# Three conv quarters exchange their tanh halves through SyncE's queue and take one in-place sum; eleven late buffers; new orders

## The chip, the cores and the metric

The kernel runs on one core of a Trainium2 chip. The metric is the device time of one execution in microseconds; the value of a version is the median over its runs. A profile is one execution recorded by the hardware profiler, with its own time beside the others.

## The reference

Pooled-key attention for 8 batches of 8 heads, then a gated feed-forward layer with a convolution of three taps along the sequence.

```python
B, H, S, D = q.shape                      # 8, 8, 576, 64
k_p = k.reshape(B, H, S // 8, 8, D).mean(axis=3)
v_p = v.reshape(B, H, S // 8, 8, D).mean(axis=3)
scores = np.matmul(q, k_p.transpose(0, 1, 3, 2)) / np.sqrt(D)
attn = softmax(scores)                    # over the 72 pooled keys
x = np.matmul(attn, v_p)                  # -> [B, S, 512]
h = np.maximum(x @ w_in, 0.0)             # [B, S, 1024]
conv_out = sum(conv_w[k] * shifted(h, k - 1) for k in range(3))
gate = 1.0 / (1.0 + np.exp(-conv_out))
out = (h * gate) @ w_out                  # float32
```

## The kernel before, in words

Batches are handled in four groups of two. Each batch goes through the same stages: its keys and values are pooled by sums, its queries are turned; its attention runs in tiles of 128 rows (scores, maximum, shift, exponential, a turn of the weights, weighted values, division, a turn of the result); then the feed-forward part runs on 1024 features in eight blocks of 128 features, called fb, and two quarters of four blocks, called f4; then the output is formed in tiles of 128 rows, copied to SBUF and stored.

A block's `ffn_in` gives h in PSUM and `ffn_relu` (ScalarE, L785) writes it to `hT`, of which there are two buffers. The convolution is made in one of two ways. In a quarter of `TAPS` VectorE makes it with two instructions a block (`ffn_tap`, L912), ScalarE squashes the result into `gT` (L922). In the other quarters TensorE makes it with small 64x64 matmuls (`ffn_conv`, L940), two blocks at a time; those come out with the two halves of partitions of one block in each pair exchanged. ScalarE writes the tanh of the straight block into the gate tile `gT` and that of the exchanged block into a helper tile `tg` (`ffn_tanh`, L965).

The sigmoid is made from a tanh with an added one; relu then carries the factor one half. `ffn_gate` adds the one and undoes the exchange: L980 adds it in place to the two straight blocks, and two instructions of 64 partitions (L982) add it while they move one half of `tg` each to the other half of `gT`. Behind that `ffn_times` (L990) multiplies the four blocks of the gate by h, which frees that part of `hT`. In a tap quarter nothing is exchanged, and a single instruction over four blocks (`ffn_tap_gate`, L927) adds the one; in batches 5 to 7 (`SIG`) ScalarE gives the sigmoid itself and no one is added.

The order of all work on all engines is written out by hand as a table: every step is an `Op` that is added to a `Graph` with the engines that can do it; `ORDER` lists the steps with the engine chosen for each (and -1 for a fill matmul that computes nothing), `FORMS` chooses between a half-array and a quarter-array form of the q and score matmuls, and `PLACES` picks each tile's buffer. Each engine, and SyncE's queue, then does its steps in that order, each waiting for what it needs.

SyncE's queue carries the loads of the first keys and queries (L300), the turn of the weights of groups 2 and 3 (`att_send`, L702: `eT` from `e`), the turn of the attention's result for batches 4 to 7 (`att_out`, L755: `xT` from `x`), the turn of the queries of group 3 (`q_send`, L554) and most stores (`ffn_store`, L1021). Output tiles of the last group go through "late" buffers, which lie in the memory of the query tiles `qp`.

Of the kernel before, what the change touches and what calls it, by code (L numbers as in the profile page):

```python
# [33 lines left out]
class Graph:  # L34
# [28 lines left out]
    CROSS = ()  # L63
    BY_TILE = ()
# [119 lines left out]
def kernel(  # L184
# [10 lines left out]
    nc = tc.nc  # L195
# [66 lines left out]
    def buf(*key):  # L262
        return buffers[key[0]][tokens[key].slots[0]]
# [1236 lines left out]
```

## Time and profile before

| what | value |
|---|---|
| median of 3 runs | 210.57 us (210.29 to 210.69) |
| the profiled execution | 210.06 us |
| its span, first to last instruction | 208.3 us |
| TensorE busy | 197.2 us (95%) |
| VectorE busy | 190.4 us (91%) |
| ScalarE busy | 174.5 us (84%) |
| GpSimd busy | 45.5 us (22%) |
| mean granted TensorE clock | 0.993 |

The span is shorter than the time by what lies around the first and the last instruction. A share of busy time is a mean over stages with different limits: what a change in one stage is worth is read from that stage. TensorE's ends are modelled, so that a busy TensorE is not TensorE at its peak. PE is TensorE, PEld its weight loads, DVE VectorE, ACT ScalarE, POOL GpSimd, SP SyncE; SPq is SyncE's queue. L numbers are lines of the kernel; in the changed kernel the same lines stand some lines lower (L980 is L982 there, L785 is L787, L990 is L999).

### The profile page before, as it was taken

The page shows a single profiled execution, that of the slowest core. Times are in us where ns is not written, and L with a number is a line of the kernel's source. Part 1 is how long each engine was busy: PE and PEld are TensorE (multiplying, and loading weights), DVE is VectorE, ACT ScalarE, POOL GpSimd, SP SyncE. Part 2 cuts the span into 40 slices and gives each one's busy share as a digit, 9 for nine tenths or more (in the row PEclk, how much of TensorE's full clock was granted, in tenths as well). Part 3 has the DMA queues.
Part 4 walks back from the last instruction along what each step waited for, and adds up shares of the span by engine and source line. Part 5 has one row for each costly group of instructions (what it writes and reads, how often), then busy time and mean ns, then how long its engine had stood idle before and what let it go on. Part 6 is the DMA issues. An engine that isn't in the chain of part 4 may idle for free.

```text
span 208.3 us, 6540 instructions
## 1 busy us (share of the span) xinstructions
PE 197.2 (95%) x2650; PEld 134.3 (64%) x2666; DVE 190.4 (91%) x338; ACT 174.5 (84%) x363; POOL 45.5 (22%) x74
## 2 busy tenths in 40 slices
PE   4999999999999999999999999999999999999990
PEld 2568688776688887666868875566556666644450
DVE  7979999889999999999999999999999999999440
ACT  3558786998899999998998999999999999797310
POOL 8553035010173211010000152040234315000000
PEclk9999999999999999999999999999999999999997
DMA  6999999999999999998497465565665557044395
GB/s 205 243 204 209 205 207 208 208 209 203 189 167 202 205 207 206 170 162 164 92 144 123 97 136 111 119 138 127 129 139 116 120 124 179 3 101 102 92 282 185
DMA packets 48835, 33.48 MB, mean 161 GB/s; under 512 B 28300, under 2 KB 43812, under 8 KB 48804
## 3 DMA queue, kind: packets, MB, share of 16 engines
q0 software_dynamic: 15216, 15.40, 45.1%
q1 hardware_dynamic: 32592, 16.20, 36.4%
q10 hardware_dynamic: 996, 1.45, 2.6%
q8 instruction: 21, 0.34, 0.6%
q14 instruction: 10, 0.08, 0.1%
HBM read 32.52 MB, written 9.44 MB: 201 GB/s over the span
## 4 chain that ended last, share of the span: by engine, by line
PE 49%; DVE 24%; ACT 16%; issue 5%; DMA 3%; SPq 0%; DVEq 0%; ACTq 0%
PE psum L776 19%; PE psum L998 13%; DVE tg L912 6%; DVE negm L634 4%; ACT x L739 4%; PE psum L718 3%; DVE gT L990 3%; DVE sd L646 3%; DMA hT<-in_k_dram 3%; PE psum L940 2%; ACT hT L785 2%; PE psum L693 2%; PE psum L608 2%; ACT gT L922 2%; ACT qT L560 2%
## 5 line engine op out<-in xcount | busy, mean ns | idle before, releaser
L776 PE MATMUL psum<-xT,w_in_sb 128*128 128x288 bf16 x512 | 70.6, 286 | 0.4
L998 PE MATMUL psum<-w_out_sb,gT 128*128 128x512 bf16 (+1 forms) x280 | 65.9, 373 | 1.1 <-issue 0.2
L776 PEld LDWEIGHTS <-w_in_sb 128*128 128x128 bf16 x512 | 48.4, 98 | 15.6 <-issue 0.6
L785 ACT ACTIVATE hT<-psum 128x576 bf16<-128x576 f32 x64 | 41.6, 671 | 4.8 <-PE psum L776 4.2
L998 PEld LDWEIGHTS <-gT 128*128 128x128 bf16 x296 | 27.7, 98 | 27.5 <-DVE gT L990 0.6
L860 POOL COPY hT<-hT 128x126 bf16<-128x126 bf16 x14 | 11.3, 810 | 84.2 <-issue 43.6
L912 DVE SCALAR_TENSOR_TENSOR tg<-hT,ratio 128x576 f32<-128x576 bf16 x36 | 28.2, 813 | 0.5 <-ACT gT L922 0.2
L634 DVE TENSOR_REDUCE negm<-psum 128x8 f32<-128x576 f32 (+2 forms) x37 | 27.4, 748 | 1.3 <-PE psum L608 0.6
L912 DVE SCALAR_TENSOR_TENSOR tg<-hT,ratio,tg 128x576 f32<-128x576 bf16 x36 | 28.2, 810 | 0.0
L922 ACT ACTIVATE gT<-tg,ratio 128x576 bf16<-128x576 f32 x36 | 27.4, 793 | 0.8 <-DVE tg L912 0.7
L990 DVE TENSOR_TENSOR gT<-gT,hT 128x2304 bf16<-128x2304 bf16 x16 | 21.4, 1348 | 0.1
L739 ACT ACTIVATE x<-psum,r 128x64 bf16<-128x64 f32 x96 | 21.2, 356 | 0.1
L1009 ACT COPY osb<-psum 128x512 f32<-128x512 f32 x27 | 16.4, 620 | 4.3 <-PE psum L998 2.7
L646 DVE TENSOR_TENSOR sd<-psum,negm 128x576 f32<-128x576 f32 x27 | 19.8, 747 | 0.1
L683 ACT ACTIVATE e<-sd 128x576 bf16<-128x576 f32 x27 | 19.4, 719 | 0.1
L718 PE MATMUL psum<-vm,eT 128*128 128x65 bf16 (+5 forms) x240 | 18.8, 222 | 0.2 <-DVE vm L516 0.2
L718 PEld LDWEIGHTS <-eT 128*128 128x128 bf16 (+1 forms) x240 | 14.8, 101 | 3.6 <-issue 0.8
L746 DVE TENSOR_TENSOR x<-psum,r 128x512 bf16<-128x512 f32 (+1 forms) x25 | 16.6, 679 | 0.2
L425 PE MATMUL psum<-gT 128*128 128x448 bf16 x40 | 12.7, 425 | 2.8 <-DVE gT L1107 2.8
L940 PE MATMUL psum<-hT,dw 64*64 64x63 bf16 (+2 forms) x448 | 13.2, 255 | 0.2 <-ACT kT L505 0.2
L512 DVE TENSOR_TENSOR v<-v 128x1280 bf16<-128x1280 bf16 (+2 forms) x24 | 12.9, 539 | 0.2
L940 PEld LDWEIGHTS <-dw 64*64 64x64 bf16 x448 | 10.9, 107 | 2.1 <-issue 1.5
(94 smaller groups left out, 236.5 us busy)
## 6 DMA issues: line engine op xcount, KB each, us to landing
out_dram<-osb SPq DMA_DIRECT2D x54, 128.0 KB, 2.4
v<-in_v_dram POOLq DMA_DIRECT2D x8, 512.0 KB, 13.7
qp<-in_q_dram POOLq DMA_DIRECT2D x7, 576.0 KB, 13.2
kk<-in_k_dram POOLq DMA_DIRECT2D x3, 1152.0 KB, 14.4
out_dram<-qp ACTq DMA_DIRECT2D x10, 128.0 KB, 3.4
hT<-in_k_dram SPq DMA_DIRECT2D x2, 576.0 KB, 5.0
w_in_sb<-in_moe_w_in_dram POOLq DMA_DIRECT2D x2, 512.0 KB, 15.4
w_out_sb<-in_moe_w_out_dram POOLq DMA_DIRECT2D x1, 1024.0 KB, 18.6
```

Source lines behind the costliest of these rows:

```text
L634: nc.vector.tensor_reduce(out=a["m"][0:rows], in_=a["s"][0:rows, :, 0:2 * KW].rearrange("p a (h s) -> p a h s", s=Sp), axis=AX.X, op=OP.ma ...
L646: nc.vector.tensor_tensor(out=a["d"][0:rows], in0=a["s"][0:rows, :, 0:2 * KW].rearrange("p a (h s) -> p a h s", s=Sp), in1=a["m"][0:rows]. ...
L683: nc.scalar.activation(out=dst, in_=src, func=ACT.Exp,)
L718: nc.tensor.matmul(out=a["o"][lo:hi, h // 4, (h % 4) * (D + 1):(h % 4 + x1 - x0) * (D + 1)], lhsT=a["eT"][:, j, lo:hi], rhs=buf("vm", b)[: ...
L739: nc.scalar.activation(out=a["x"][0:rows, n * D:(n + 1) * D], in_=ov[:, n // 4, n % 4, 0:D], func=ACT.Identity, scale=r[0:rows, n // 4, n ...
L776: nc.tensor.matmul(out=banks(ps)[:, j, 0:SC], lhsT=w_in_block(dc, fb), rhs=buf("xT", g)[:, dc, i * S + j * SC:i * S + (j + 1) * SC], start ...
L785: nc.scalar.activation(out=h_of(b)[:, fb].rearrange("p (a s) -> p a s", a=2), in_=banks(ps)[:, :, 0:SC], func=ACT.Relu, scale=1.0 if (b, f ...
L912: nc.vector.scalar_tensor_tensor(out=acc, in0=h, scalar=w, in1=acc if tap else mid, op0=OP.mult, op1=OP.add)
L922: nc.scalar.activation(out=gate, in_=acc_of(b, fb, ps), func=squash(b, fb), scale=ratio[:, 1, fb:fb + 1])
L940: nc.tensor.matmul(out=banks(pss[r ^ c])[c * D:(c + 1) * D, j, lo:hi], lhsT=dw[r * D:(r + 1) * D, tap * n_fb + fb, :], rhs=hT[r * D:(r + 1 ...
L990: nc.vector.tensor_tensor(out=gate, in0=gate, in1=h_of(b)[:, four], op=OP.mult)
L998: nc.tensor.matmul(out=bank(ps)[0:rows, columns], lhsT=buf("gT", g)[:, fb, t * P:t * P + rows], rhs=w_out_sb[:, fb, columns], start=(fb == 0),
```

## The change

Three of the quarters that TensorE convolves, (2, 0), (2, 1) and (3, 0) as (batch, quarter), get another gate. The two exchanged halves of `tg` are moved into `gT` by two DMAs on SyncE's queue (`ffn_cross`), as soon as the tanh of both exchanged blocks are written; then `ffn_tap_gate` adds the one to all four blocks in place with one VectorE instruction, behind all four tanh and the DMAs. The four other convolved quarters keep `ffn_gate`. The late buffers grow from 8 to 11, the three new ones in the memory of the value tiles `v`; a copy into a late buffer also waits until the pooled values of batches 4 to 7 are made. `ORDER`, `FORMS` and `PLACES` are new throughout.

```diff
+    SWAP = ((2, 0), (2, 1), (3, 0))
...
     ORDER = (
-        0, 16, 4, 24, 12, 44, 28, 8, 10, 14, 32, -1, -1, 42, 36, -1, -1, 40, -1, -1,
+        0, 16, 4, 24, 8, 12, 44, 48, 14, 42, 10, 64, -1, -1, 3, -1, 32, -1, -1, 38,
...
-             "hT": 2, "gT": 2, "xT": 2, "qT": 3, "kk": 1, "qp": 4, "v": 3, "vm": 5, "kT": 5, "sd": 3, "r": 3, "s": 2, "late": 8}
+             "hT": 2, "gT": 2, "xT": 2, "qT": 3, "kk": 1, "qp": 4, "v": 3, "vm": 5, "kT": 5, "sd": 3, "r": 3, "s": 2, "late": 11}
...
     half_qp = [t.rearrange("p h s -> p (h s)")[:, i * 1024:(i + 1) * 1024] for t in buffers["qp"] for i in range(2)]
+    half_qp += [t.rearrange("p j x -> p (j x)")[:, 0:1024] for t in buffers["v"]]
...
+    def ffn_cross(b, f4):
+        g, i = where[b]
+        tg, gate = buf("tg", b, f4), buf("gT", g)[:, 4 * f4:4 * f4 + 4, i * S:(i + 1) * S]
+        gate = gate.rearrange("p (f e) s -> p e f s", e=2)
+        for r in range(2):
+            nc.sync.dma_start(out=gate[r * D:(r + 1) * D, 1], in_=tg[(1 - r) * D:(2 - r) * D])
...
+            elif f2 % 2 and (b, f4) in Graph.SWAP:
+                o = add({"SP": 1.3}, w, lambda f4=f4: ffn_cross(b, f4), after=[tanh[f4][1], tanh[f4][3]], uses=tg + [gtok[g]], land=(2.4, 0, 1))
+                need = [o] + tanh[f4]
+                if (b, f4) not in Graph.SIG:
+                    need = [add(dve(0.78), w + 6 * f2 + Graph.GATE, lambda f4=f4: ffn_tap_gate(b, f4), after=need, uses=[gtok[g]])]
+                gated = add(dve(1.39), w + 6 * f2 + Graph.GATE, lambda f4=f4: ffn_times(b, f4), after=need, uses=[htok[b], gtok[g]])
+                gdone.setdefault(b, []).append(gated)
...
-            osb, free = (token("late", g, t), [x for n in range(4, B) for x in qdone[n, 0]]) if g == 3 else (token("osb", g, t), [])
+            osb, free = (token("late", g, t), [x for n in range(4, B) for x in qdone[n, 0] + [vdone[n]]]) if g == 3 else (token("osb", g, t), [])
```

Where the tables move the instructions is seen best on three engines. On VectorE, at the gates of batch 3, the order before reads (a row is the line, the operation, out<-in with buffer numbers, and partitions x elements):

```order
L980 TENSOR_SCALAR gT_122<-gT_122 128x2x576
L982 TENSOR_SCALAR gT_122<-tg_118 64x2x576 x2
L731 RECIPROCAL r_113<-psum 128x8
L912 SCALAR_TENSOR_TENSOR tg_119<-hT_116,ratio,tg_119 128x576
L990 TENSOR_TENSOR gT_122<-gT_122,hT_116 128x4x576
L516 TENSOR_TENSOR vm_90<-v_88,mask_wide 128x15x64
L927 TENSOR_SCALAR gT_122<-gT_122 128x4x576
L990 TENSOR_TENSOR gT_122<-gT_122,hT_116 128x4x576
```

and now, for the same batch, whose h lies in the other buffer:

```order
L929 TENSOR_SCALAR gT_122<-gT_122 128x4x576
L514 TENSOR_TENSOR v_89<-v_89 128x5x256
L999 TENSOR_TENSOR gT_122<-gT_122,hT_117 128x4x576
L733 RECIPROCAL r_113<-psum 128x8
L748 TENSOR_TENSOR x_107<-psum,r_113 128x512
L636 TENSOR_REDUCE negm_95<-psum 128x8
L929 TENSOR_SCALAR gT_122<-gT_122 128x4x576
L648 TENSOR_TENSOR sd_129<-psum,negm_95 128x576
L733 RECIPROCAL r_113<-psum 128x8
L748 TENSOR_TENSOR x_110<-psum,r_113 128x512
L999 TENSOR_TENSOR gT_122<-gT_122,hT_117 128x4x576
```

The tap quarter now comes first and the exchanged quarter, with its single sum, second, and attention work stands between the sum and the product. On SyncE's queue, around the second turn of queries, the order before reads:

```order
L554 DMA_TRANSPOSE qT_79<-qp_76 128x18x128
L1021 DMA out_dram<-osb_126 64x512 x2
L755 DMA_TRANSPOSE xT_114<-x_107 128x4x128
L702 DMA_TRANSPOSE eT_104<-e_103 128x5x128
L702 DMA_TRANSPOSE eT_105<-e_101 128x5x128
L755 DMA_TRANSPOSE xT_114<-x_110 128x4x128
L554 DMA_TRANSPOSE qT_80<-qp_75 128x18x128
L702 DMA_TRANSPOSE eT_104<-e_102 128x5x128
```

and now:

```order
L556 DMA_TRANSPOSE qT_80<-qp_74 128x18x128
L704 DMA_TRANSPOSE eT_106<-e_101 128x5x128
L556 DMA_TRANSPOSE qT_81<-qp_77 128x18x128
L993 DMA gT_122<-tg_118 64x2x576 x2
L704 DMA_TRANSPOSE eT_104<-e_102 128x5x128
L757 DMA_TRANSPOSE xT_114<-x_109 128x4x128
L757 DMA_TRANSPOSE xT_114<-x_108 128x4x128
L757 DMA_TRANSPOSE xT_114<-x_107 128x4x128
L704 DMA_TRANSPOSE eT_105<-e_103 128x5x128
L993 DMA gT_122<-tg_120 64x2x576 x2
```

The two turns of queries stand closer together, and the first exchange (L993) is right behind the second. On ScalarE, where the next batch's first relu goes into the buffer that batch 3 leaves, the order before reads:

```order
L965 ACTIVATE gT_122<-psum 128x576
L785 ACTIVATE hT_116<-psum 128x576
L683 ACTIVATE e_101<-sd_129 128x2x2x144
L965 ACTIVATE tg_120<-psum 128x576
L965 ACTIVATE gT_122<-psum 128x576
```

and now:

```order
L787 ACTIVATE hT_116<-psum 128x576
L787 ACTIVATE hT_117<-psum 128x576
L967 ACTIVATE gT_122<-psum 128x576
L967 ACTIVATE tg_119<-psum 128x576
L787 ACTIVATE hT_117<-psum 128x576
```

In both the relu into the freed buffer stands ahead of the last two tanh of batch 2.

More of the change, by code (lines that the diff above doesn't have):

```diff
@@ L72 @@
     ORDER = (
[55 rows of a table removed]
[55 rows of a table added]
     )
     FORMS = (
-        1, 1, 1, 0, 0, 1, 1, 0, 0, 0, 1, 1, 0, 1, 1, 0, 0, 0, 1, 1, 1, 0, 1, 1, 1, 0, 0, 1, 0, 1, 0, 1, 1, 1, 1, 1, 1, 1, 0, 0,
+        1, 0, 1, 0, 0, 1, 1, 0, 0, 0, 1, 1, 1, 0, 0, 0, 0, 0, 1, 1, 0, 0, 1, 0, 0, 0, 0, 1, 1, 0, 0, 1, 0, 0, 0, 1, 1, 0, 1, 0,
     )
     PLACES = (
[18 rows of a table removed]
[18 rows of a table added]
     )
```

144 rows, old and new, of tables (ORDER, PLACES) are left out of this document.

## The prediction

> **What bounds the kernel now.** I read the page's head first, then busy time by stretch, then the chain of waits.
>
> ```profile
> span 208.3 us, 6540 instructions
> ...
> PE 197.2 (95%) x2650; PEld 134.3 (64%) x2666; DVE 190.4 (91%) x338; ACT 174.5 (84%) x363; POOL 45.5 (22%) x74
> ```
>
> The columns of the stretches are: length, then busy time and (instructions) of PE, PEld, DVE, ACT and POOL, the granted clock, the DMA share, GB/s.
>
> ```profile
> 47.00:95.00 48.00, 47.36 (x797) 34.81 (x799) 47.35 (x84) 45.65 (x90) 9.93 (x20) 1.00 1.17 191
> 95.00:128.00 33.00, 32.56 (x497) 23.94 (x499) 32.62 (x59) 31.05 (x72) 4.65 (x8) 1.00 0.67 121
> 128.00:154.00 26.00, 25.69 (x248) 15.59 (x251) 26.00 (x42) 25.86 (x69) 5.49 (x8) 1.00 0.59 126
> 154.00:194.00 40.00, 39.58 (x247) 23.73 (x250) 39.59 (x53) 36.47 (x77) 8.21 (x8) 1.00 0.48 106
> ```
>
> From 47 to 194 us VectorE is busy 47.35 + 32.62 + 26.00 + 39.59 = 145.56 of 147 us: 1.44 us idle in all. TensorE reads 145.19 of 147, but its ends are modelled. ScalarE is full only in 128 to 154 (25.86 of 26). Outside this stretch VectorE has slack only ahead of 47 us.
>
> ```profile
> 1.83 6.32 DMA hT<-in_k_dram
> 8.17 1.16 ACT kk L307
> 9.37 0.75 PE psum L432 x18
> ...
> 148.57 1.31 ACT x L739 x4
> ...
> 182.80 8.83 DVE tg L912 x12
> 191.63 2.55 DVE gT L990 x2
> 194.23 8.84 PE psum L998 x48
> ```
>
> The chain (start, length, what) begins with the load of the first keys and their cast, passes ScalarE's divides (L739) around 148 us, and ends in the last twelve taps, two products and the 48 matmuls that need those products. After 203.07 us only a copy and stores follow. So the end stands where VectorE's last product stands (194.18), plus a tail of 14.1 us that the change can hardly touch: five tiles need the last product in both versions. What VectorE does before that product, and how long it waits, decides the time.
>
> **The change part by part.** The three quarters first.
>
> ```profile
> L980 DVE TENSOR_SCALAR gT<-gT 128x1152 bf16<-128x1152 bf16 x7 | 3.3, 465 | 0.0
> ...
> L982 DVE TENSOR_SCALAR gT<-tg 64x1152 bf16<-64x1152 bf16 x14 | 6.4, 455 | 0.2
> ...
> L927 DVE TENSOR_SCALAR gT<-gT 128x2304 bf16<-128x2304 bf16 x3 | 2.2, 748 | 0.0
> ```
>
> By busy time over count, a quarter's gate was one L980 and two L982, 3.3/7 + 2 x 6.4/14 = 1.39 us; it becomes one L927, 2.2/3 = 0.73. Three quarters: -1.97 us of VectorE, all of it between 103 and 121 us, where VectorE is full. That is the gain on the path, if nothing takes its place.
>
> Something does. The new order gives VectorE work that was ScalarE's.
>
> ```profile
> L746 DVE TENSOR_TENSOR x<-psum,r 128x512 bf16<-128x512 f32 x23 | 15.3, 679 | 0.2
> L771 DVE COPY xT<-psum 128x512 bf16<-128x512 bf16 x1 | 0.4, 426 | 0.6 <-PE psum L763 0.6
> L707 DVE COPY eT<-psum 128x640 bf16<-128x640 bf16 x3 | 1.4, 477 | 0.0
> L307 DVE CAST kk<-hT 128x1152 bf16<-128x1152 f32 x1 | 0.9, 921 | 0.0
> L739 ACT ACTIVATE x<-psum,r 128x64 bf16<-128x64 f32 x96 | 21.2, 356 | 0.1
> L771 ACT COPY xT<-psum 128x512 bf16<-128x512 bf16 x16 | 9.1, 587 | 1.6 <-PE psum L763 1.5
> ```
>
> VectorE gets one divide more (15.3/23 = 0.67), three full xT copies (3 x 0.4) and a half one (some 0.3), and one raw cast of 512 columns (0.9 x 512/1152 = 0.4): +2.6. It loses one eT copy (1.4/3 = 0.47) and a half-width q copy (about the same): -0.9. Net of the gates, 2.6 - 0.9 - 1.97 = **-0.3 us** of VectorE work ahead of the last product. With errors of a tenth or so in each of eight items I hold it for anything between -0.6 and +0.3.
>
> ScalarE loses eight divide pieces (8 x 21.2/96 = 1.77), three xT copies (3 x 9.1/16 = 1.71) and smaller pieces on both sides that cancel: about -3.3 us. It does not set the end by itself, so this is worth only what VectorE and TensorE waited for it. In the full stretch VectorE has 1.44 us of waits altogether. I take a fifth of them, **-0.3**; the ends are -1.44 (all waits go) and the rivals below (new ones come).
>
> The head: the second half of the first keys is cast on VectorE (0.92) where the chain shows ScalarE's 1.16: **-0.2**. It is worth that only if VectorE is free at 8.17 us, and nothing if it is not.
>
> ```profile
> 2.49 0.24 DVE L1107 MEMSET gT<- 128x224 uint32 x1
> ...
> 7.07 1.15 DVE L382 COPY mask_wide<-mask 128x960 bf16<-128x960 bf16 x1
> ```
>
> ```profile
> 2.79 5.15 PE L425 MATMUL psum<-gT 128*128 128x448 bf16 x14 [2.79 <-DVE gT L1107]
> ```
>
> One thing speaks against the head. The widened mask (L382, 1.15 us) now stands ahead of the clearing (L1107) that the first fill matmuls wait for, so they start some 1.2 us later, and there are 8 and not 14. The 14 took 5.15 us, 0.37 each, though the granted clock reads full there:
>
> ```profile
> PEclk9999999999999999999999999999999999999997
> ```
>
> ```profile
> 73.06 0.38 PE psum L425 x2
> ```
>
> Later fills of the same shape step at 0.38/2 = 0.19 on the chain. If eight fills leave TensorE as quick as fourteen did, this costs 0; if the first transposes and key matmuls run at the slow step, 34 of them lose some 0.05 each up to 9 us, most of it ahead of the second cast, and at most 0.4 us reaches the path. I take 0. The Trainium skill, in "TensorE: Matmul & The Clock Gate", Part 1: The HAM clock gate, says that the first 3.4 us or so of matmuls run at half clock whatever their number, in a window that runs free of the kernel; by that rule the start of full speed moves with the first fill and the sum would be 0.4 worse. The fill's slow steps agree with that; the granted clock row does not show it.
>
> TensorE gets more work: two q transposes change from the small to the full form, six tiles of scores likewise.
>
> ```profile
> L608 PE MATMUL psum<-kT,qT 64*64 64x72 bf16 x408 | 8.1, 200 | 0.2
> ...
> L542 PE MATMUL psum<-ident,qp 128*64 128x128 bf16 x126 | 4.6, 220 | 0.1
> ...
> L621 PE MATMUL psum<-kT,qT 128*128 128x144 bf16 x40 | 4.3, 226 | 0.4 <-ACT e L683 0.3
> ...
> L546 PE MATMUL psum<-ident,qp 64*64 64x64 bf16 x180 | 2.5, 195 | 0.0
> ```
>
> A set of 36 L546 costs 2.5/5 = 0.5, its 18 L542 4.6/7 = 0.66; a tile of 16 L608 0.32, its four L621 0.43: 2 x 0.16 + 6 x 0.11 = +1.0 us. By the order most of it falls before 110 us, where fill matmuls still pad TensorE's gaps, so I cost it at nothing; if TensorE is what the middle waits for, it costs the whole 1.0.
>
> The exchange itself: six issues on SyncE's queue, and a landing ahead of each sum.
>
> ```profile
> eT<-e SPq DMA_TRANSPOSE x18, 2.6
> ...
> qT<-qp SPq DMA_TRANSPOSE x2, 6.1
> ```
>
> No row shows a plain on-chip copy. By size (147 KB beside 164 KB) it is nearest to the eT row, 2.6 us; the qT row, 6.1, is the upper end. Queued behind each sum on VectorE is everything, first of all the maxima that release the exponentials. Adding up both orders row by row at the groups' steps, the last tanh of each quarter stands some 11, 6.6 and 7 us ahead of its sum. With 1.2 us of issue and 2.6 of landing about 3 us are left over: cost 0, as long as the queue is in time.
>
> The late buffers rise from eight to eleven: in the tail of before, copies wait for TensorE and not for a buffer, so 0. The stores' last issues keep their place.
>
> **The sum.** -0.3 - 0.3 - 0.2 = -0.8 us against the profiled execution's 210.06 us (span 208.3 and 1.76 around it), 209.3; the median of the runs is 0.51 higher, so **209.8 us**. About 0.2% (0.4 us) is what a measurement of this kernel can tell from no change.
>
> **The rivals.** *Turnover of hT, slower.* Only two hT buffers exist; a batch's first relu waits until the products of the batch two before are done.
>
> ```profile
> 108.00 1.36 DVE L990 TENSOR_TENSOR gT<-gT,hT 128x2304 bf16<-128x2304 bf16 x1
> ```
>
> ```profile
> 115.23 0.65 ACT L785 ACTIVATE hT<-psum 128x576 bf16<-128x576 f32 x1
> ```
>
> In before the second product of batch 3 ends at 109.36 and the next relu into that buffer runs at 115.23: 5.9 us to spare. The new order puts about 5.1 us more VectorE work ahead of that product (an estimate, summed row by row), since the exchanged quarter's sum comes late, and 1.5 us less ScalarE work ahead of the relu. That leaves -0.7. If both engines keep their pace, ScalarE stands 0.7 us at its relu and TensorE behind it, its two-bank sums unread; TensorE's 1.0 us is then uncovered too: -0.5 + 0.7 + 1.0 = +1.2, **211.8 us**. Against it: ScalarE has 3.3 us less to do. It decides once the product is later than the relu.
>
> *SyncE's queue, slower.* Start and length of SyncE's issues:
>
> ```profile
> 82.15 6.36 SPq L702 DMA_TRANSPOSE eT<-e  x3
> ...
> 91.67 2.80 SPq L554 DMA_TRANSPOSE qT<-qp  x1
> ...
> 102.79 3.83 SPq L554 DMA_TRANSPOSE qT<-qp  x1
> ...
> 112.00 1.42 SPq L1021 DMA_DIRECT2D out_dram<-osb  x2
> ...
> 123.89 1.25 SPq L702 DMA_TRANSPOSE eT<-e  x1
> ```
>
> From the first of these to the end of the last (43 us) the 17 merged rows sum to 38.9 us: 90% full. To the same eleventh eT the new order has three crosses more (3 x 1.2) and one store pair and one xT fewer (-2.5): +1.1 of 4.1 us left. But both qT issues (2.8 and 3.8) now stand close together right ahead of the first cross, with an eT and three xT behind it. If that bunch runs 2 to 3 us late, the weighted values wait for eT, and past 3 us the sums wait too: -0.5 + 2.5 = +2.0, **212.6 us**. For it: the 90%. Against it: the distances above.
>
> *Slow start or a used-up ledger, no change.* The slow start alone gives 209.8 + 0.4 = 210.2; VectorE's ledger at its upper end (+0.3 for -0.3) gives 210.4; both give **210.8 us**. All lie within the bound of no change.
>
> **How the numbers follow.** Forecast (faster by over 0.2%) 0.46, slow start or used-up ledger (no change) 0.18, turnover 0.20, SyncE's queue 0.16: slower 0.36. The lower end takes all of VectorE's 1.44 us of waits in place of 0.3: 209.8 - 1.1 = 208.7. The upper end lies between the two slower rivals, at 212.2; it leaves out the worse half of the queue's case and little below.
>
> **What would show it.** Right: VectorE's three sums at 0.73 each and no L984 on those quarters; VectorE over 98% busy from 47 us to its last product, at about 193.4; ScalarE near 171 us busy; the 48 last matmuls right behind the product. Wrong: VectorE idle by more than 3 us in the middle, with L999 or the sum waiting for a DMA (queue), or ScalarE's relu (L787) idle for a VectorE product near 114 us (turnover); or first fills that are slow up to 9 us and a first key matmul later than 9.4 us.

## The result, and the profile after

The changed kernel takes **213.09 us** (median of 4 runs, 212.39 to 213.37) against 210.49 of the kernel before on the same chip: ratio 1.0119, 95% interval 1.0091 to 1.0146. It is 2.6 us slower, and lies 0.9 us above the upper end of the predicted range. The profiled execution took 212.9 us.

The head of the page of the changed kernel:

```profile
span 211.2 us, 6334 instructions
...
PE 197.3 (93%) x2541; PEld 135.1 (64%) x2558; DVE 191.3 (91%) x337; ACT 172.7 (82%) x353; POOL 38.8 (18%) x72
```

The span is 2.9 us longer. VectorE's last product shows where that splits. In the chain of the changed kernel (start, length, what) it ends at 195.27; before, at 194.18:

```profile
193.94 1.33 DVE gT L999
195.27 0.60 DVE qp L1018
195.88 0.61 DVE osb L1018
...
196.50 4.11 DMA out_dram<-osb
...
200.63 3.90 DMA out_dram<-osb
...
205.13 0.59 ACT v L1018
...
205.77 1.05 PE psum L1007 x8
...
206.91 0.42 DVE qp L1018
```

So +1.1 us stand ahead of the last product, and behind it the tail grew from 14.1 to 15.9 us: **+1.8**. Before, the chain went from the product straight into 48 matmuls that ended 8.9 us later; now it goes through stores, a copy on ScalarE and eight late matmuls, which end 11.6 us later.

Ahead of the product, busy time by stretch (columns as before), first of the kernel before, then of the changed one:

```profile
0.00:47.00 47.00, 43.06 (x821) 31.62 (x822) 41.21 (x100) 33.75 (x57) 17.16 (x30) 1.00 1.16 211
47.00:194.18 147.18, 145.31 (x1785) 98.08 (x1798) 145.74 (x234) 139.04 (x305) 28.29 (x44) 1.00 0.77 140
```

```profile
0.00:47.00 47.00, 41.86 (x737) 31.08 (x738) 40.51 (x100) 33.57 (x55) 17.01 (x30) 1.00 1.15 208
47.00:195.27 148.27, 146.39 (x1756) 99.44 (x1772) 146.77 (x232) 137.94 (x297) 21.80 (x42) 1.00 0.80 144
```

VectorE's work up to its last product is 187.28 us for 186.95, +0.33. Its idle time is 6.49 for 5.79 us ahead of 47 us (+0.70), and 1.50 for 1.44 behind it (+0.06). Ahead of 47 us most of it lies between 25 and 35 us, where VectorE is busy 7.98 us for 9.36 and waits for TensorE, which it did not before (first the kernel before, then the changed one and its waits there):

```profile
25.00:35.00 10.00, 9.99 (x159) 8.33 (x158) 9.36 (x23) 7.97 (x14) 4.25 (x6) 1.00 1.24 206
```

```profile
25.00:35.00 10.00, 10.00 (x141) 7.92 (x137) 7.98 (x21) 8.84 (x14) 0.81 (x2) 1.00 1.24 206
```

```profile
DVE negm L636 <- PE psum L623: 0.8, 1, 0.8
DVE eT L709 <- PE psum L695: 0.8, 1, 0.8
```

That stretch has 1.38 us more idle time, the first 10 us have 0.50 more, and the rest of the 47 us has 1.18 less.

The gates did what the prediction said: six L929, three of them new, at 0.75 us. The four sums L982 of the quarters that were not changed take 0.62 us each, where the seven of before took 0.47 (3.3/7). The raw cast that came over from ScalarE stands below them:

```profile
L929 DVE TENSOR_SCALAR gT<-gT 128x2304 bf16<-128x2304 bf16 x6 | 4.5, 750 | 0.0
...
L982 DVE TENSOR_SCALAR gT<-gT 128x1152 bf16<-128x1152 bf16 x4 | 2.5, 620 | 0.0
...
L309 DVE CAST qp<-hT 128x512 bf16<-128x512 f32 x1 | 0.6, 633 | 0.6 <-DMA hT<-in_q_dram 0.6
```

The tail's waits behind 190 us, in the changed kernel (line, waited for: us in total, times, longest); before, VectorE's copies there waited for TensorE alone:

```profile
ACT qp L1018 <- DMA out_dram<-qp: 7.5, 1, 7.5
DVE qp L1018 <- DMA out_dram<-qp: 7.4, 3, 3.1
...
PE psum L1007 <- ACT v L1018: 2.5, 1, 2.5
ACT v L1018 <- DMA out_dram<-osb: 2.0, 1, 2.0
```

```profile
DVE qp L1009 <- PE psum L998: 5.9, 4, 3.1
```

ScalarE's part of the tail, and SyncE's queue (start, length):

```profile
195.11 7.39 ACTq L1030 DMA_DIRECT2D out_dram<-qp  x8
202.59 0.58 ACT L1018 COPY qp<-psum 128x512 f32<-128x512 f32 x1 [7.51 <-DMA out_dram<-qp]
```

```profile
190.70 11.54 SPq L1030 DMA_DIRECT2D out_dram<-osb  x10
```

Three things meet here. ScalarE has eight store issues ahead of its copies of tiles 6 and 7, and they hold it for 7.39 us, 0.92 each with the gaps between them. The late buffers of tiles 0 and 1 are given to tiles 5 and 4 again, and the first of them also to tile 8, though five of the eleven stay unused, so VectorE's copies wait for stores. And on SyncE's queue two finished tiles (copied by 190 us) stand behind a store whose copy VectorE makes at 195.88, after its last product.

### The profile page after: what moved, and what is told of

Same layout as the page of the kernel before. It is cut to its first block, busy times and chain, and to the rows that moved or that the text cites. A ratio compares the mean times of both kernels' runs of the same rounds, so it can differ in the third digit from the quotient of the medians.

```text
span 211.2 us, 6334 instructions
## 1 busy us (share of the span) xinstructions
PE 197.3 (93%) x2541; PEld 135.1 (64%) x2558; DVE 191.3 (91%) x337; ACT 172.7 (82%) x353; POOL 38.8 (18%) x72
## 4 chain that ended last, share of the span: by engine, by line
PE 65%; ACT 14%; DMA 8%; DVE 6%; issue 4%; SPq 1%; ACTq 0%; DVEq 0%
PE psum L778 27%; PE psum L1007 16%; DMA out_dram<-osb 5%; PE psum L720 4%; PE psum L942 4%; DMA hT<-in_k_dram 3%; ACT x L741 3%; PE psum L695 2%; ACT gT L924 2%; PE psum L623 2%; PE psum L427 2%; PE psum L544 2%; ACT hT L787 2%; ACT osb L1018 2%; PE psum L610 2%
## 5 line engine op out<-in xcount | busy, mean ns | idle before, releaser
L862 POOL COPY hT<-hT 128x126 bf16<-128x126 bf16 x13 | 6.2, 480 | 89.5 <-ACT hT L787 63.8
L685 ACT ACTIVATE e<-sd 128x576 bf16<-128x576 f32 x27 | 18.6, 695 | 1.1 <-DVE sd L648 0.9
L741 ACT ACTIVATE x<-psum,r 128x64 bf16<-128x64 f32 x88 | 19.2, 359 | 0.1
L748 DVE TENSOR_TENSOR x<-psum,r 128x512 bf16<-128x512 f32 (+1 forms) x26 | 17.7, 685 | 0.4
L720 PEld LDWEIGHTS <-eT 128*128 128x128 bf16 (+1 forms) x240 | 15.3, 100 | 4.2 <-issue 0.8
L1018 ACT COPY osb<-psum 128x512 f32<-128x512 f32 x26 | 15.9, 623 | 0.9 <-PE psum L1007 0.5
L942 PE MATMUL psum<-hT,dw 64*64 64x288 bf16 (+1 forms) x448 | 13.1, 256 | 0.5 <-ACT hT L787 0.4
L562 ACT COPY qT<-psum 128x1152 bf16<-128x1152 bf16 (+2 forms) x11 | 10.6, 985 | 3.5 <-PE psum L544 2.9
## 6 DMA issues: line engine op xcount, KB each, us to landing
qp<-in_q_dram POOLq DMA_DIRECT2D x7, 576.0 KB, 14.1
```

What stands on the lines that cost most here:

```text
L720: nc.tensor.matmul(out=a["o"][lo:hi, h // 4, (h % 4) * (D + 1):(h % 4 + x1 - x0) * (D + 1)], lhsT=a["eT"][:, j, lo:hi], rhs=buf("vm", b)[: ...
L741: nc.scalar.activation(out=a["x"][0:rows, n * D:(n + 1) * D], in_=ov[:, n // 4, n % 4, 0:D], func=ACT.Identity, scale=r[0:rows, n // 4, n ...
L942: nc.tensor.matmul(out=banks(pss[r ^ c])[c * D:(c + 1) * D, j, lo:hi], lhsT=dw[r * D:(r + 1) * D, tap * n_fb + fb, :], rhs=hT[r * D:(r + 1 ...
L1018: copy(out=osb[0:rows, columns], in_=bank(ps)[0:rows, columns])
```

## The experiments

Each was timed beside the kernel before on the same chip (210.5 to 210.7 us throughout). Ratios are to that. In the diffs, `ORDER` holds twice a step's number, plus one where the second possible engine is chosen.

**The tail, one mend at a time.** Distinct late buffers:

```diff
+    PLACES = PLACES[:-8] + (0,) + PLACES[-7:-5] + (4,) + PLACES[-4:-1] + (7,)
```

> The changed kernel with the last three tiles' late buffers made distinct (tile 5 in 0, tile 4 in 4, tile 8 in 7, where it has 3, 5 and 3 a second and third time). Tail of the changed kernel: 15.9 us from VectorE's last product to the span's end, 14.1 before the change; 213.1 us against 210.5. Theory A, buffers used again: VectorE's copies no longer wait for a store (three waits, 7.4 us, go), the bank comes free sooner, and the time falls by 0.8 to 1.5, to 211.6 to 212.3. Theory B, ScalarE stuck in its queue issues: VectorE's waits go, but the copy of tile 7 on ScalarE still comes at 205, the last eight matmuls behind it: 212.8 to 213.1. Theory C, the stores' bytes: DMA engines are full from 200 us on, so nothing changes: 213.1.

213.93 us, 1.0144 (1.0117 to 1.0171). VectorE's waits for stores are gone, the last eight matmuls still stand 2.4 us behind ScalarE: B's picture, and no gain. The median lies above what all three theories gave it, and 0.8 us above the changed kernel's, though the intervals overlap.

The two finished stores ahead (steps 738 and 869, ahead of 750):

```diff
+    for n, m in ((738, 750), (869, 750)):
+        _o.remove(2 * n); _o.insert(_o.index(2 * m), 2 * n)
```

> The changed kernel with two stores on SyncE's queue moved ahead: tile 0 and tile 8 of the third group, copied by 189 us, stand behind the store of tile 5, which VectorE copies at 195.8; here they stand ahead of the store of tile 3. DMA engines are idle from 182 to 190 us in the changed kernel. Theory C, the stores' bytes (0.5 MB more are left after 190 us than before the change, 1.8 us at 290 GB/s): 0.5 MB leave the full stretch and the time falls by 1.3 to 1.8, to 211.3 to 211.8. Theory A, buffers: stores finish somewhat sooner and so do the reused buffers: 212.5 to 212.9. Theory B, ScalarE stuck in its issues: they wait for lanes that come free sooner: 212.3 to 212.9.

212.82 us, 1.0106 (1.0085 to 1.0126): what A or B gave it, not C.

ScalarE's two copies on VectorE:

```diff
+    ORDER = tuple({2 * 1040 + 1: 2 * 1040, 2 * 1044 + 1: 2 * 1044}.get(n, n) for n in ORDER)
```

> The changed kernel with the PSUM copies of the fourth group's tiles 6 and 7 on VectorE, where ScalarE does them behind 8 store issues that take 7.4 us. Theory B: the last matmuls no longer wait for ScalarE; TensorE ends 2 us sooner and the time falls by 1.2 to 1.8, to 211.3 to 211.9. Theory A, buffers: VectorE takes the copies in turn behind the copy that waits for its buffer until 203.9, so they come no sooner: 212.8 to 213.3. Theory C, the stores' bytes: 213.1.

213.05 us, 1.0114 (1.0095 to 1.0134): as A said, the copies now wait behind the copy that waits for its buffer. C gave the same time; the next run tells against it.

All three:

> The changed kernel with all three: distinct late buffers, the two finished stores ahead, and the copies of tiles 6 and 7 on VectorE. If the tail's loss (15.9 for 14.1 us) is these three together, the time is 213.1 - 1.8 = 211.3, with VectorE's last product where it was (195.3). If the tail is bound by something else, such as the rate at which the last stores land whatever their order, it stays over 212.5. The other 1.1 us, by which the last product comes later than before the change, stay in any case: under 210.8 would contradict that.

**211.60 us**, 1.0054 (1.0033 to 1.0076). The 48 last matmuls are again one piece right behind the product, as in the chain before the change:

```profile
195.91 8.91 PE psum L1013 x48
```

No mend alone gave anything that can be told from the changed kernel; the three together give 1.5 us. In the profile the tail is 14.0 us, as long as before the change, and the last product ends 0.6 us later than in the changed kernel (195.85). Each wait stood behind another that ended at nearly the same time.

**The exchange apart from the order.** The new order with the old three instructions in all three quarters:

```diff
-  lambda f4=f4: ffn_cross(b, f4), ...  lambda f4=f4: ffn_tap_gate(b, f4)
+  lambda: None, ...                    lambda f4=f4: ffn_gate(b, f4)
```

> The changed kernel with its new order kept and the exchange alone taken back: the three quarters are summed by the old three instructions, and SyncE issues no exchange. Base: the changed kernel's 213.1 us. Theory X, the exchange gains what VectorE saves (3 x 0.66 = 1.97 us) and the loss comes from the new order: 214.4 to 215.1. Theory Y, the exchange pays its gain back on SyncE's queue, whose issues from 105 to 142 us stand nearly end to end (a late third exchange lets the sum wait 0.3 to 0.9 us in three of five traces): 212.6 to 213.6.

214.81 us, 1.0189 (1.0160 to 1.0218): theory X. In the new order the exchange gains 1.7 us; the order by itself costs 4.2 (the kernel before took 210.57 beside it).

The old order with the exchange, two sums moved down:

```diff
+            if halves.count((b, fb // 4)) == 2:
+                ffn_cross(b, fb // 4)
...
+    for n, m in ((457, 458), (465, 466)):
```

> The kernel before with the exchange alone: its own order, each exchange issued right behind the later of its two tanh halves, and the two sums of batch 2 moved down VectorE's order to stand right ahead of their products (in place they would follow their last tanh within 2 us, where an exchange takes 1.2 us of issue and 2.5 of landing). Base: 210.5 us. Theory X, the exchange gains what VectorE saves: 208.6 to 209.5. Theory Y, the queue takes it back (before, SyncE issues fill 38.9 of 43 us from 82 us on; six issues more are 3.7 us): 210.3 to 212.0, with sums that wait for the exchange or weighted values late.

217.58 us, 1.0340 (1.0296 to 1.0385): neither. Its waits and SyncE's queue show a cost that neither theory had:

```profile
DVE tg L917 <- DMA gT<-tg: 5.1, 1, 5.1
```

```profile
119.03 1.33 SPq L707 DMA_TRANSPOSE eT<-e  x1
120.46 1.36 SPq L760 DMA_TRANSPOSE xT<-x  x1
121.92 1.25 SPq L988 DMA_DIRECT2D gT<-tg  x2
```

A tap of VectorE, which the edit left where it was, writes the `tg` buffer that the third exchange is still to read. The exchange turns the release of a buffer from VectorE's own order into the landing of a DMA, and that DMA stood behind two sends. This wait is 5.1 of the 9.6 us by which VectorE idles more behind 47 us; the rest was not followed up. So the old order cannot take the exchanges of batch 2 without more moves.

The one exchange that it can take:

```diff
+    SWAP = ((3, 0),)
```

> The kernel before, its order unchanged, with one quarter exchanged: quarter 0 of batch 3, whose last tanh stands some 5 us of VectorE's work ahead of its sum there; in the run with three exchanges in this order its sum waited for nothing. Theory X: VectorE saves 0.66 us and the time falls by 0.4 to 0.7, to 209.8 to 210.2. Theory Y: SyncE, with two issues (1.3 us) more among the sends, delays an eT or xT by as much: 210.4 to 211.5.

211.04 us, 1.0019 (0.9999 to 1.0039): theory Y by the median, though the interval just reaches no change. In its profile (an execution of 211.8 us) TensorE waits 0.8 us for an xT send, and VectorE's last product comes 1.1 us later than in the kernel before although VectorE has 0.66 us less to do:

```profile
PE psum L777 <- DMA xT<-x: 0.8, 1, 0.8
```

```profile
192.65 2.62 DVE L1007 TENSOR_TENSOR gT<-gT,hT 128x2304 bf16<-128x2304 bf16 x2
```

**SyncE's queue in the new order.** The traces with three exchanges come in two kinds. In the profiled execution of the changed kernel no sum waits. In four of the five later runs with these three exchanges, whose mends of tail and head touch nothing there, a sum and a copy wait. The rows of the one with distinct late buffers, for VectorE, ScalarE and TensorE:

```profile
DVE gT L930 <- DMA gT<-tg: 0.9, 1, 0.9
```

```profile
ACT osb L1019 <- DMA out_dram<-osb: 0.7, 1, 0.7
```

```profile
PE psum L1008 <- ACT osb L1019: 1.0, 2, 0.9
```

The third sum waits for its exchange, and ScalarE at 131 us for an output buffer whose store SyncE issued late. Two small mends in the middle:

```diff
+    for n, m in ((467, 468),):
...
+    PLACES = tuple({528: 4, 541: 3, 601: 3}.get(i, p) for i, p in enumerate(PLACES))
```

> The changed kernel with the three mends of the tail (211.6 us) and two in the middle: the third sum stands one maximum later on VectorE, and ScalarE's copy at 131 us takes an output buffer whose store was issued earlier (three places change). Theory Y, SyncE's late issues cost part of the middle (VectorE waited 0.3 to 0.9 us for the third exchange and ScalarE 0.6 to 1.2 for an output buffer, TensorE 0.7 to 1.1 behind it, in three traces of five, whose last product came 0.6 to 1.6 us later than in the two without): 210.7 to 211.1, and both waits gone. If the lateness only shows at the next place, 211.4 to 211.8.

212.83 us, 1.0105 (1.0067 to 1.0143), on top of the tail's mends: by the median worse than without (211.60), though the runs scatter from 211.59 to 214.65 and the intervals overlap. Both waits are gone, and a later output buffer is waited for instead:

```profile
ACT osb L1029 <- DMA out_dram<-osb: 1.6, 1, 1.6
```

The exchanges on GpSimd's queue (on top of the mends of the tail and of the head, below):

```diff
-            nc.sync.dma_start(out=gate[...], in_=tg[...])
+            nc.gpsimd.dma_start(out=gate[...], in_=tg[...])
```

> The changed kernel with the mends of tail and head (211.1 us) and the exchanges issued on GpSimd's queue, which issues nothing else then, in place of SyncE's, where six issues are 3.9 us between 105 and 122 us. Theory Y, SyncE's lateness is what is left over the kernel before: the waits for the third exchange (0.4) and for an output buffer at 131 us (ScalarE 1.0, TensorE 0.9) go, VectorE's last product comes 0.5 to 1.0 us sooner: 210.1 to 210.6. If the lateness is not SyncE's own but that of the exponentials it sends, 211.0 to 211.4. If GpSimd's queue is slow to start a copy, the sums wait for it, and it is over 211.6.

212.36 us, 1.0072 (1.0049 to 1.0095): the third case. From there the copy lands in 4.1 us at the median, 5.3 at the most (2.5 and 3.8 from SyncE), and a sum waits:

```profile
DMA to landing us min/median/max: 2.9/4.1/5.3
```

```profile
DVE gT L941 <- DMA gT<-tg: 2.5, 1, 2.5
```

The Trainium skill, in "DMA: Bandwidth & Descriptors", SWDGE vs HWDGE vs iDMA, says that DMAs issued from GpSimd have their descriptors built in software and start more slowly than SyncE's. The landings agree, by 1.6 us.

The third exchange alone taken back:

```diff
+  lambda f4=f4: ffn_cross(b, f4) if (b, f4) != (2, 1) else None
+  lambda f4=f4: (ffn_gate if (b, f4) == (2, 1) else ffn_tap_gate)(b, f4)
```

> The same mends (211.1 us), with the third exchange (quarter 1 of batch 2) taken back: that quarter is summed by the old three instructions. VectorE has 0.66 us more, SyncE two issues (1.3 us) fewer from 120 us on. Theory X, VectorE's work alone counts: 211.6 to 211.8. Theory Y, SyncE's lateness costs what the third exchange saves: 210.6 to 211.2, with no wait for an output buffer at 131 us.

**210.50 us**, 0.9990 (0.9978 to 1.0002): theory Y, just below its range. The third exchange saves 0.66 us of VectorE and costs more; in the trace without it nothing waits for an exchange or an output buffer. The 12 runs lie within 210.22 to 210.99, where the 12 with three exchanges lie within 210.37 to 212.38. That the third exchange makes the scatter is not shown: two exchanges without the mend of the head, further down, scatter from 210.50 to 211.92.

No exchange, with the same mends:

> The new order with the mends of tail and head and no exchange at all (three quarters summed by the old three instructions). With three exchanges this was 211.1 us, with two 210.5. Theory X, each exchange saves its 0.66 us of VectorE: 2 x 0.66 over the 210.5, 211.6 to 212.0. Theory Y, the other two exchanges also cost on SyncE's queue: 210.3 to 211.2.

212.89 us, 1.0104 (1.0083 to 1.0125). The other two exchanges gain 2.4 us, more than X's 1.3. The two profiled executions lie 2.0 us apart: VectorE's work up to its last product accounts for 1.46 of them (189.48 for 188.02 us), its idle time for 0.15 and the tail for 0.4 (13.4 for 13.0).

**The head.** The kernel before's start (the clearing ahead of the widened mask, 14 fills):

```diff
+    for n, m in ((5, 24),):
...
+    ORDER = ORDER[:13] + (-1,) * 6 + ORDER[13:]
+    PLACES = PLACES[:3] + (0, 5, 6, 0, 5, 6) + PLACES[3:]
```

> The changed kernel with the three mends of the tail (211.6 us) and the kernel before's start: the blank tile cleared ahead of the widened mask, and 14 first fill matmuls for 8. VectorE idles 0.7 us more before 47 us in the changed kernel than before it. Theory H, the first key matmuls run slow since the fills start a microsecond late (18 in 1.29 us, 0.75 before): they return to 0.75 and the time falls by 0.3 to 0.7, to 210.9 to 211.3. Theory O, the head loses time through the order of what follows, not through the fills: 211.4 to 211.8, with the idle time before 47 us still over 6.2 us.

211.14 us, 1.0029 (1.0008 to 1.0050). TensorE's start in the changed kernel, then in this one, and then in the run with the tail's three mends, which has the changed kernel's start:

```profile
3.80 3.17 PE L427 MATMUL psum<-gT 128*128 128x448 bf16 x8 [3.80 <-DVE ident_k L387]
6.90 1.06 PE L544 MATMUL psum<-ident,qp 128*64 128x128 bf16 x16
7.75 1.29 PE L434 MATMUL psum<-gT,kk 128*64 128x144 bf16 x18
9.23 0.86 PE L434 MATMUL psum<-gT,kk 128*64 128x144 bf16 x18 [0.18 <-DVE kk L309]
```

```profile
2.79 5.39 PE L439 MATMUL psum<-gT 128*128 128x448 bf16 x14 [2.79 <-DVE gT L1128]
8.11 0.64 PE L556 MATMUL psum<-ident,qp 128*64 128x128 bf16 x16
8.58 1.60 PE L446 MATMUL psum<-gT,kk 128*64 128x144 bf16 x36
```

```profile
6.90 0.69 PE L550 MATMUL psum<-ident,qp 128*64 128x128 bf16 x16
7.42 0.73 PE L440 MATMUL psum<-gT,kk 128*64 128x144 bf16 x18
```

The transposes and the first keys are quick with the mend, but they are also quick in the third trace, without it: how long the slow steps last differs from execution to execution. The last key matmul ends at 10.18 us, no sooner than the 10.09 of the changed kernel, since the second cast sets it. VectorE's idle time ahead of 47 us stays at 6.6 us, and 2.12 of it lie between 25 and 35 us as in the changed kernel (2.02): theory O for the place. The medians nevertheless fell by half a microsecond, so it was tried again with two exchanges and without the head's mend:

> The version with two exchanges and the tail's mends, without the mend of the head (8 first fills behind the widened mask, as the change has them); with the mend of the head it was 210.5 us. Theory H, the head's mend is worth what the medians showed with three exchanges (211.6 to 211.1): 210.9 to 211.2. Theory O, the fills' slow start reaches nothing, since VectorE idled 6.6 us before 47 us with the mend too, and the half microsecond was scatter of the run with three exchanges: 210.3 to 210.7.

211.25 us, 1.0020 (1.0005 to 1.0034), 0.75 above the same with the mend. By the median this is H; but the profiles show the last product at the same place (it starts at 193.09 here, at 193.26 with the mend) and 1.1 us between the tails instead, 14.1 and 13.0. The traces hint at how the start can reach the stores at the end. The store issues from 196 to 200 us, first without the mend of the head, then with it (shortest, median and longest in ns):

```profile
L1036 ACTq DMA_DIRECT2D out_dram<-qp x5: 473/607/1932, 195.5 to 199.6; - x5
L1036 SPq DMA_DIRECT2D out_dram<-osb x2: 466/1258/2050, 196.9 to 197.4; - x2
```

```profile
L1042 ACTq DMA_DIRECT2D out_dram<-qp x6: 483/592/804, 195.7 to 199.2; - x6
L1042 SPq DMA_DIRECT2D out_dram<-osb x2: 466/534/603, 197.1 to 197.6; - x2
```

Without the mend one issue on each queue takes about 2 us, and both end at 199.5. The trace has a load of instructions (queue q8) that starts at 197.50, beside them; with the mend, which adds six fills at the start, that load starts at 193.83. In all 17 traces, each of the 36 store or exchange issues behind 60 us that took over 1.2 us overlaps such a load. That the load holds the issues is read from this coincidence; no run moved a load alone, so the head's share stays open.

**Work handed back.** Three copies on ScalarE again:

```diff
+    ORDER = tuple({980: 981, 1002: 1003, 272: 273}.get(n, n) for n in ORDER)
```

> The version with two exchanges and the mends (210.5 us), with three copies handed back from VectorE to ScalarE as before the change: two half xT tiles at 74 us (0.76 us of VectorE together) and a half q copy at 90 us (0.5). ScalarE is busy 44.0 of 48 us there, VectorE 47.2. Theory L, the work that the new order moves to VectorE counts in full: 1.2 us less, 209.2 to 209.8. Theory W, ScalarE's relief mattered as much as VectorE's work (the prediction counted on it): 210.2 to 210.8.

211.50 us, 1.0044 (1.0028 to 1.0061): further than W, a loss of 1.0 us. In the profile VectorE has 1.6 us less work up to its last product (186.44 for 188.02) and idles 2.35 us more. It waits for scores instead; that ScalarE, with more to do, is what delays them is likely, but was not traced:

```profile
DVE negm L649 <- PE psum L636: 2.0, 2, 1.2
```

**The kernel before with the tail's mends.** Step 862 ahead of 850, tile 5's copy on VectorE, its own buffer:

```diff
+    for n, m in ((862, 850),):
...
+    ORDER = tuple({2 * 1033 + 1: 2 * 1033}.get(n, n) for n in ORDER)
+    PLACES = PLACES[:-3] + (4,) + PLACES[-2:]
```

> The kernel before with the tail's three mends alone: the store of the third group's tile 7, copied by 190 us, moved ahead of the store of tile 4, which is copied at 194; the copy of the fourth group's tile 5 on VectorE and in a late buffer of its own. Theory A-B-C of the tail holds for the kernel before too, whose ScalarE copy at 202.2 stands behind issues: 209.6 to 210.2. If its tail was free of these waits, as the prediction held: 210.4 to 210.7.

**209.55 us**, 0.9959 (0.9939 to 0.9979): faster than both kernels, at the lower end of what was expected. Its seven runs fall into four from 209.29 to 209.55 and three from 210.21 to 210.61, so the median is uncertain by more than half a microsecond. In the tail before, ScalarE copied tile 5 between its issues; now VectorE does, half a microsecond sooner:

```profile
202.19 0.59 ACT L1009 COPY qp<-psum 128x512 f32<-128x512 f32 x1 [5.32 <-PE psum L998]
```

```profile
201.65 0.69 DVE L1015 COPY qp<-psum 128x512 f32<-128x512 f32 x1 [0.17 <-PE psum L1004]
```

## Why the prediction was wrong

- *The tail, "which the change can hardly touch": the step that failed, and the largest.* It was sized at nothing and measured +1.8 us in the profiles; the three mends give back 1.5. The late buffers were costed from the waits of before, "copies wait for TensorE and not for a buffer, so 0", and "the stores' last issues keep their place". But the change also gave out these buffers anew, put copies on ScalarE behind store issues, and put finished stores behind an unfinished one. The trace of before could not show waits that the new order makes; the order of the tail's copies and issues had to be read for them. And the tail was not free of such waits before either: mended there, it gave 1.1 us by the medians (0.4 to 1.3 by the interval), about the whole gain of 0.8 that was forecast.
- *Three gates, -1.97.* Right: 0.75 us measured for 0.73, and 1.7 us gained on the path in the new order.
- *The ledger, -0.3.* +0.33 measured, just past its upper bound. The largest miss is in instructions that the ledger took as unchanged: the four sums L982 took 0.62 us for 0.47, 0.6 in all. Two of the four are long, 0.84 us at 72.04 and 0.74 at 84.21. GpSimd issues a DMA during both (71.59 to 72.62, and from 83.93 on); that this is the reason is not shown. Beside that a raw cast of 512 columns took 0.63 for the 0.4 scaled from a longer one, and a kT cast is longer (0.5 for 0.3); against that, the scaled identity (L387) took 0.12 for 0.49. One copy for the tail's third group went to VectorE too, but behind the last product.
- *Fewer waits behind 47 us, -0.3.* +0.06. ScalarE's relief was perhaps not worthless: when three copies were handed back to it, VectorE idled 2.35 us more. It may have been needed to keep the waits where they were.
- *The head, -0.2.* VectorE idles 0.70 us more ahead of 47 us, and the prediction looked for it in the wrong place: the first 10 us account for 0.50, and from 25 to 35 us, which no term of the sum covers, it idles 1.38 more. There TensorE is busy 10.00 of 10.00 us and does no fill, in either kernel; which step of the new order makes VectorE wait was not tested. At the start, the second key cast on VectorE took 0.77 us for 1.16, but its load landed 0.24 us later and the key matmuls behind it took 0.86 for 0.75, so the last of them ended where it did before (10.09 for 10.12). The slow first steps were counted at 0 for the path; the keys' end at 10.09 us with them and at 10.18 without bears that out, though the medians leave a doubt.
- *The exchange's DMAs at 0.* The landing was sized well (2.5 us at the median for 2.6). The queue was in time in the profiled execution and in one of the five later ones: over all, the third exchange costs more than it saves, the rival of SyncE's queue in small.
- *Turnover of hT.* It did not happen: no relu waits for a product near 114 us in the trace.
- *TensorE's +1.0 at nothing.* Its busy time up to the last product is 188.25 for 188.37 us, 1.08 more behind 47 us and 1.20 less ahead of it. Behind 47 us VectorE's waits grew by 0.06 only. But the prediction's reason, that fills still pad TensorE's gaps before 110 us, does not hold everywhere: from 25 to 35 us there are no fills, and VectorE waits for TensorE.

The order alone can be added up in the profile of the run without exchanges (215.4 us, the longest of its six). Up to the last product VectorE has 2.0 us more work there than in the kernel before (188.97 for 186.95) and 1.2 more idle time, and the tail is 2.2 longer (16.3): 5.4 us of span. By the medians the order costs 4.2. Against it stands the exchange's 1.7. The prediction had the work (its +2.6 and -0.9) and the exchange; the tail it took for nothing, and the idle time for a small gain.

## What to carry to other kernels

A change that needs a new order has two prices, and the edit itself may be the smaller. Read the new order where the kernel drains: for each engine that both computes and issues stores, what computation stands behind an issue, which buffers come round again though others are free, and which finished store stands behind an unfinished one. A single mend there shows nothing while a second wait ends at the same time, so mend them together before the place is called innocent.

Moving data by a DMA in place of an instruction also moves the release of the source buffer into that queue, so it pays only where the queue has slack behind it: of three like exchanges in the new order, two paid and the third cost more than it saved.

## What the runs showed of the hardware

- An engine's DMA issues hold back its own computation: eight stores took 7.39 us of ScalarE's time, 0.92 each, where a single issue takes 0.47 at the least. One of the eight started when VectorE's copy of its tile had ended (200.85 behind 200.79), and one took 1.87 us from 197.28. What the others wait for the trace does not name; the DMA engines moved 119 GB/s from 195 to 200 us and 273 GB/s from 200 to 205.
- In 17 traces each of the 36 store or exchange issues behind 60 us that took over 1.2 us overlapped a load of instructions (queue q8); the 1.87 us issue above stands beside one that starts at 197.09. The longest issue away from such loads took 1.16 us.
- A copy of 144 KB from one part of on-chip memory to another lands in 2.5 us from SyncE's queue and in 4.1 from GpSimd's (medians).
- TensorE's slow first steps lasted 3.0 to 5.9 us behind the first fill in the eight traces with 8 fills, and 4.1 to 5.4 in the nine with 14. The Trainium skill, in "TensorE: Matmul & The Clock Gate", Part 1: The HAM clock gate, gives some 3.4 us of time whatever the number of matmuls, in a window that runs free of the kernel's start. The runs agree that it is not a number (8 slow matmuls in one trace, 46 in another, both with 8 fills) and that it varies with nothing changed at the start, and most show a longer time.
